# A DeltaNet-and-MLP kernel: x·w_in by eleven products of tiles instead of twelve, with shared sums on GpSimd

## The chip, the core and the metric

The kernel runs on one core of a Trainium2 chip. The core has engines that work side by side and wait for each other by semaphores: TensorE (PE in the profile; PEld is its weight load), VectorE (DVE), ScalarE (ACT), GpSimd (POOL) and the queue that issues most transfers (SP). Each engine takes its own instructions in the order in which the program wrote them. TensorE writes into PSUM; here DVE and ACT take results out of PSUM, and GpSimd works on SBUF alone.

The metric is the device time of one execution, in microseconds (us). Before the change three runs gave 692.02, 690.9 and 692.4, median 692.02.

## What is computed

```python
# attention: B, H, S, D = 4, 8, 768, 48, a state matrix per (batch, head)
for t in range(S):
    y[:, :, t] = q_t @ state
    state += beta_t * outer(k_t, v_t - state^T k_t)       # k normalised
# MLP on the 3072 tokens x 384 features of y
h = x @ w_in                                               # 384 -> 2048
g = h * clip(h + 3, 0, 6) / 6                              # hardswish
out = g @ w_out                                            # 2048 -> 384
```

## The kernel before, in words

**Attention.** The 768 steps are cut into 24 chunks of 32 tokens; one chunk of all four batches fills 128 partitions. For a chunk `t`, `prep` (L474) scales the keys on GpSimd (`kb`, L479), makes the mask times beta there (`mb`, L457), transposes k and q on TensorE (L495), multiplies them (`sc`, L516), lets DVE cut out the triangles `L` and `LB` (L527), and lets GpSimd make `bkb` (L467). Chunks are inverted in groups of four: `inverse` (L715) is a long chain of DVE instructions on two SBUF tiles (`pr` L728 and `A` L733, 60 of them, with a transpose of about 2 us at either end, L447 and L451). `chain` (L756) is the recurrence: `ks` (L775), `R` on DVE (L788), `pz` (L877), `Z` on ACT (L882), `su` and `py` on TensorE, the state on DVE (L908), and the output rows `y` (DVE L788 and L831), turned by TensorE (`yt`, L841) into `xT`, the input of the MLP.

**MLP.** Two chunks make a block of 256 tokens; there are 12 blocks, counted from 0 in the code. `up(blk)` (L935) makes h^T: for each of 16 slices of 128 features, three fp32 products of a 128x128 weight tile with 256 columns of `xT`. The profile counts two matmul instructions for each fp32 product. ACT makes relu(h/6 + 1/2) (L955) and DVE min(·,1)·h (L958), into `g`. `down_by_seven(blk)` (L1032, from block 2) makes g·w_out by seven products of half matrices instead of eight, each of 8 products of 192 columns (L1052). It needs 16 sums of halves of g (L1038, 128x256, two SBUF inputs), made on DVE between the products, and combines the results in `o` (L1059, L1062). Products are made in the order 4, 2, 1, 5, 7, 6, 3. PSUM for all this is a ring of four banks (`pm`); `ks`, `su` and `sc` have two others (`pc`).

**Order.** Everything is recorded in program order by hand. Up to chunk 4 the string `ORDER` (L22) names the pieces one by one. Then the loop at L1262 runs a step for each chunk from 5 on: 15 units, each of which takes pieces of the chain and of `prep` by the table `plan`, one unit of `mlp_units` (L1117: `down` of a block and `up` of the next, 30 units together), and two or three pieces of the running inverse or norms. `prep` runs six chunks ahead, so after chunk 17 it has nothing more to do; the last block's `up` and `down` stand alone at the end. The inverse of the next group starts in the second step of a group of four, fills the third and ends in the fourth.

```python
            for u in range(NU):
                if u in plan:
                    plan[u]()
...
                take(units)
                settle(1)
...
                take(fill, 2 + (u % 3 == 0))
```

Of the kernel before, what the change touches and what calls it, by code (L numbers as in the profile page):

```python
# [35 lines left out]
x4 a*2 u b6 x4 q a u c*2 u ru c w ru a gu u p8 a u gu a q*2 n9 k q c a u a w c p6 ru q s c p7 p6  # L36
m7 a p7 u m8 k c h3 u ru gu b7 p8 h3 p8 c k h4 p8 gu c*2 p8 a u h4 ru gu u k ru gu u y4 p8 x4*2 u
y4 p8 i2*2 u i2 v i2*3 ru i2 u a i2*2 gu a ru u i2*3 h4 i2 gu b8 i2 k n9 q i2*2 k u q k*2 v k*2 ub
k*2 v h4 i2*2 u rb i2 gb n9 i2 u i2 v i2 ru i2 gu i2 u ru i2*3 v q gu i2 c n9 u k i2 u i2 u ru gu
q ru i2 gu i2 k n9 v i2 u h4 y4 i2 v*2 i2 n9 u y4 i2 q u*2 i2 u n9 ru i2*3 q k gu q*2 i2 n9 q i2*3  # L40
n9 u k n9 q e i2*4 ru u gu y4 h4 e n9 u y4 k n9 k*2 i2 k*5 i2*2 k*3 ru k ru gu i2 u gu p9 u e i2 u
i2*5 e u i2*4
"""


# [1 line left out]
def kernel(  # L47
# [62 lines left out]
        return 0 if g == 0 else G0 + (g - 1) * GS  # L110


    NKB, NQB, NBKB, NLB, NKQ = 2, 4, 8, 8, 7
    kbufs = [persist.tile([P, H, DP], FP32, name=f"kb{i}") for i in range(NKB)]
    qbufs = [persist.tile([P, H, DP], FP32, name=f"qb{i}") for i in range(NQB)]
    bkbufs = [persist.tile([P, H, DP], FP32, name=f"bkb{i}") for i in range(NBKB)]
    kfs, vfs = {}, {}

    def tokens(ap, b, t):
# [5 lines left out]
    def needs(*what):  # L125
        assert past.issuperset(what), (what, set(what) - past)
# [33 lines left out]
                    past.add(("q", t))  # L160
                yield

    NVF = 3

    def load_v(t):
        if t < N:
# [284 lines left out]
        nc.vector.transpose(out=turn(inverted(g)), in_=problems(A))  # L451

    def mask(t):
        mb = mbs[t] = work.tile([P, 2, NP, 2, C], FP32, name="mb")
        needs("beta")
        for e in range(2):
            nc.gpsimd.tensor_tensor(  # L457
                out=mb[:, e],
                in0=beta_tok[:, t, e:H:2].unsqueeze(2).unsqueeze(3).to_broadcast([P, NP, 2, C]),
                in1=mask2[:].unsqueeze(1).to_broadcast([P, NP, 2, C]),  # L460
                op=ALU.mult,
            )
        yield

    def scaled(t):
        needs(("kb", t), *pad(t), *([("bkb", t - NKB)] if t >= NKB else []))
        nc.gpsimd.tensor_tensor(  # L467
            out=bkbufs[t % NBKB][:, :, 0:D], in0=kbufs[t % NKB][:, :, 0:D],
            in1=beta_tok[:, t, 0:H].unsqueeze(2).to_broadcast([P, H, D]), op=ALU.mult,
        )  # L470
        past.add(("bkb", t))
        yield
# [65 lines left out]
    def product(t):  # L538

        assert G == 8 and C == 4 * G and 4 * H * C == NP * B * 2 * C
        needs("blocks")
        LT = X(t)
        by = "p (h w) -> p h w"

        ring("KQ", NKQ, ("x", t))
        VYTF = work.tile([P, 4, H * C], FP32, name="VY", tag="KQ", bufs=NKQ)  # L550
        VY, V, Y, T, F = VYTF[:, 0:2], VYTF[:, 0, :], VYTF[:, 1, :], VYTF[:, 2, :], VYTF[:, 3, :]

        keys = []

        def times(rhs):

            n = rhs.shape[1]
            key = ("pi", t, len(keys))
            ring("pm", NPM, key)
            keys.append(key)  # L560
            ps = psM.tile([P, 2, H * C], FP32, name="pi", tag="pm")
            for h in range(H):
                w = slice(C * h, C * h + C)
                for b in range(B):
                    nc.tensor.matmul(
                        ps[rows(b), 0:n, w], lhsT=T[rows(b), w], rhs=rhs[rows(b), :, w],
                        start=True, stop=True, skip_group_check=True,
                        tile_position=(C * b, C * b),
                    )
            return ps  # L570

        def plus(ps):
            nc.vector.tensor_tensor(out=Y, in0=Y, in1=ps, op=ALU.add)

        nc.vector.tensor_tensor(
            out=V.rearrange("p (h n w) -> p h n w", h=H, w=G),
            in0=LT.rearrange("p h (n w) -> p h n w", w=G),
            in1=blocks[:].unsqueeze(1).unsqueeze(3).to_broadcast([P, H, C // G, G]),
            op=ALU.mult,
        )  # L580
        nc.vector.transpose(out=T, in_=V)
        yield
        ps = times(VY[:, 0:1, :])
        yield
        nc.vector.tensor_tensor(
            out=Y.rearrange(by, w=C), in0=eye[:].unsqueeze(1).to_broadcast([P, H, C]),
            in1=V.rearrange(by, w=C), op=ALU.subtract,
        )
        nc.vector.tensor_tensor(
            out=F.rearrange(by, w=C), in0=LT, in1=V.rearrange(by, w=C), op=ALU.subtract  # L590
        )
        yield
        nc.scalar.activation(out=V, in_=ps[:, 0, :], func=ACTF.Copy)
        yield
        nc.vector.transpose(out=T, in_=ps[:, 0, :])
        read(*keys)
        yield
        ps = times(VY)
        yield
        nc.vector.transpose(out=T, in_=ps[:, 0, :])  # L600
        plus(ps[:, 1, :])
        read(*keys)
        yield
        ps = times(VY[:, 1:2, :])
        yield
        plus(ps[:, 0, :])
        nc.vector.transpose(out=T, in_=Y)
        read(*keys)
        yield
        ps = times(F.unsqueeze(1))  # L610
        yield
        nc.scalar.activation(out=V, in_=ps[:, 0, :], func=ACTF.Copy)
        yield
        nc.vector.transpose(out=T, in_=ps[:, 0, :])
        read(*keys)
        yield
        ps = times(VY)
        yield
        nc.vector.transpose(out=T, in_=ps[:, 0, :])
        nc.vector.tensor_tensor(out=Y, in0=Y, in1=ps[:, 1, :], op=ALU.subtract)  # L620
        read(*keys)
        yield
        ps = times(VY[:, 1:2, :])
        yield
        nc.vector.scalar_tensor_tensor(
            out=LT, in0=Y.rearrange(by, w=C), scalar=-1.0,
            in1=ps[:, 0, :].rearrange(by, w=C), op0=ALU.mult, op1=ALU.subtract,
        )
        read(*keys, ("x", t))
        past.add(("X", t))  # L630
        yield
# [3 lines left out]
    def join(t):  # L635
# [4 lines left out]

        needs("corner")
        LT = X(t)
        ring("KQ", NKQ, ("x", t))
        tiles = work.tile([P, 4, H, C], FP32, name="VY", tag="KQ", bufs=NKQ)
        T, S, T2 = (tiles[:, i] for i in range(3))

        def times(name, m, k):
# [108 lines left out]
    def chain(t, whole=True):  # L756
# [5 lines left out]
        KQ, LB = KQs.pop(t), LBs[t]  # L762
        if t > 0:
            needs(("state", t - 1))
        bkb = bkbufs[t % NBKB]

        def of_state():
            ph = [banks("ks", t, i) for i in range(2)]
# [91 lines left out]
        if t == 0:  # L860
            R = vfl
        else:
            needs("parity")
            Rt = work.tile([P, DM], FP32, name="R", bufs=1)
            for x, ph, into in ((0, even, vfl), (1, odd, Rt[:])):
                plus(Rt[:], ph, parity[:, x, 0:1], into)
            R = Rt[:]
            yield
# [9 lines left out]
        past.add(("pz", t))  # L878
        yield 1
        read(("pz", t))  # L880
        Zt = work.tile([P, DM], FP32, name="Z", bufs=1)
        nc.scalar.activation(out=Zt[:], in_=pz[:, 0:DM], func=ACTF.Copy)  # L882
        Z = zs[t] = Zt[:]
        past.add(("Z", t))
# [15 lines left out]

        needs(("bkb", t))
        su = update() if t < N - 1 else []
        if whole:
            take(outs[t])
        yield
# [29 lines left out]
    def up(blk, half_of=None):  # L935
# [5 lines left out]
        for f in range(NFC):  # L941
# [27 lines left out]
                past.add(("up", blk))  # L969
            yield  # L970

    def to_dram(t, o):
        for b in range(B):
            r0 = b * S + t * C
            eng = nc.scalar if t >= N - CB and b % 2 else nc.sync
            eng.dma_start(out=out[r0 : r0 + C, :], in_=o[rows(b ^ 1)])
# [55 lines left out]
    def down_by_seven(blk):  # L1032
# [2 lines left out]

        def sums(op, out, a, b, fs):
            for f in fs:
                nc.vector.tensor_tensor(out=A(f, *out), in0=A(f, *a), in1=A(f, *b), op=op)  # L1038

        lo, hi, A11, A12, A21, A22 = (0, 2), (4, 6), (0, 0), (0, 1), (1, 0), (1, 1)  # L1040
        o = mlp.tile([128, CB, DM], FP32, name="o", bufs=1)
# [20 lines left out]
            nc.vector.tensor_tensor(out=out, in0=a, in1=b, op=ALU.add)  # L1062

        settle()
        product(4, A22, T4, 0)
        yield
        product(4, A22, T4, 1)
        copy(C21, 4, -1.0)
        yield
        product(2, A12, B21, 0)  # L1070
        yield
        product(2, A12, B21, 1)
        copy(C11, 2)
        sums(ALU.add, A22, A21, A22, lo)
        yield
        product(1, A11, B11, 0)
        sums(ALU.add, A22, A21, A22, hi)
        yield
        product(1, A11, B11, 1)
        copy(u, 1)  # L1080
        sums(ALU.subtract, A21, A11, A21, lo)
        yield
        product(5, A22, T1, 0)
# [33 lines left out]
    def mlp_units():  # L1117
# [3 lines left out]
        for f in range(0, NFC, WF):  # L1121
# [3 lines left out]
            for _ in range(WF):  # L1125
                next(u1)
                yield
        for blk in range(1, N // CB):
            if blk < FIRST:
                for c in range(CB):  # L1130
                    for f in range(0, NFC, WF):
                        if c == 0:
                            needs(*(("read", ("ph", blk, f + i, None)) for i in range(2)))
                        down(blk, c, f)
                        yield
            else:
                yield from down_by_seven(blk)
            if blk + 1 < N // CB:
                for n, _ in enumerate(up(blk + 1)):
                    if blk + 1 == FIRST and n >= HF:  # L1140
                        drain(rest)
                        if n % 2:
# [15 lines left out]
            pass  # L1158

    NU = 15  # L1160
    LA = 6
    LE = 4
    LS = G0 + GS
    gens = {}

    def made(name, make, ok=True):
# [177 lines left out]
```

## Time and profile before

The profiled execution took 688.24 us; its span, from the first to the last instruction, is 686.5 us, so 1.7 us lie around it.

| engine | busy us | share of the span | instructions |
|---|---|---|---|
| TensorE (PE) | 647.2 | 94% | 11208 |
| weight load (PEld) | 567.8 | 83% | 11208 |
| VectorE (DVE) | 467.8 | 68% | 1210 |
| ScalarE (ACT) | 238.9 | 35% | 476 |
| GpSimd (POOL) | 95.2 | 14% | 147 |

In the views below a row of the timeline reads: start in us, duration in us, engine, line, operation, output<-input, shape, how many were merged into the row, and in brackets how long the engine sat idle before it and what released it. Rows of one engine can overlap by a few hundredths, and matmuls by more, because they are pipelined: the pace of a run of matmuls is taken from start to start, not from one duration.

### The profile page before, as it was taken

Reading aid. Unit: us, or ns where it says so; the run is one execution under the profiler, and the core shown is the slowest. Engines: PE = TensorE matmul, PEld = TensorE weight load, DVE = VectorE, ACT = ScalarE, POOL = GpSimd, SP = SyncE. Lnnn points to the kernel's source line nnn. Section 1 sums busy time; section 2 is a strip of 40 time slices with the busy share of each in tenths; the row PEclk is TensorE's granted clock in tenths of the full one; section 3 lists DMA queues with packets and bytes.
Section 4 is the critical chain, followed back from the end, with each engine's and each line's share of the span. In section 5 each row is a group of like instructions: output and inputs, shape, how many; then the busy total and the mean of one; then the engine's idle time right before and its main releaser. Section 6 shows DMA issues by size and latency. Waiting matters only on the chain.

```text
span 686.5 us, 25308 instructions
## 1 busy us (share of the span) xinstructions
PE 647.2 (94%) x11208; PEld 567.8 (83%) x11208; DVE 467.8 (68%) x1210; ACT 238.9 (35%) x476; POOL 95.2 (14%) x147
## 2 busy tenths in 40 slices
PE   2668989999999999999999999999999999999997
PEld 2458877776688988988988988988988989989997
DVE  5898776888746997846985745985546985445242
ACT  5995677421233232232232232232232132132220
POOL 6241022203521100400101302100000000000000
PEclk9977899999999999999999999999999999999999
DMA  7987125412041030031030030020020020000000
GB/s 197 246 199 189 37 66 139 82 24 47 15 79 30 2 68 6 2 78 29 3 64 9 3 71 2 2 61 1 3 48 2 2 48 2 25 3 1 25 0 24
DMA packets 88494, 33.20 MB, mean 48 GB/s; under 512 B 80160, under 2 KB 83232, under 8 KB 88384
## 3 DMA queue, kind: packets, MB, share of 16 engines
q1 hardware_dynamic: 88128, 31.29, 20.5%
q8 instruction: 88, 1.44, 0.9%
q10 hardware_dynamic: 256, 0.30, 0.2%
q14 instruction: 22, 0.18, 0.1%
HBM read 26.84 MB, written 4.72 MB: 46 GB/s over the span
## 4 chain that ended last, share of the span: by engine, by line
PE 73%; DVE 12%; DMA 7%; issue 3%; ACT 2%; SPq 1%; POOL 0%; DVEq 0%; ACTq 0%; POOLq 0%
PE ph L947 33%; PE po L1052 21%; PE po L987 4%; PE ks L775 3%; PE py L796 2%; PE su L893 2%; PE pz L796 2%; DVE g L1038 2%; DMA w_out<-in_moe_w_in_dram 2%; DVE pr L728 2%; DVE A L733 2%; PE sc L516 2%; PE pt L495 2%; DMA spare<-in_moe_w_in_dram 2%; DMA qb<-in_q_dram 1%
## 5 line engine op out<-in xcount | busy, mean ns | idle before, releaser
L947 PE MATMUL ph<-xT,w_in 128*128 128x256 f32 (+1 forms) x1248 | 271.3, 371 | 3.8 <-DVE g L958 2.3
L947 PEld LDWEIGHTS ph<-xT,w_in 128*128 128x128 f32 x1248 | 222.3, 194 | 33.1 <-DVE g L958 3.5
L955 ACT ACTIVATE g<-ph,halves 128x256 f32<-128x256 f32 (+1 forms) x208 | 94.4, 456 | 198.1 <-PE ph L947 196.5
L958 DVE SCALAR_TENSOR_TENSOR g<-g,ph 128x256 f32<-128x256 f32 (+1 forms) x208 | 81.7, 396 | 100.1 <-ACT g L955 99.9
L1052 PE MATMUL po<-w_out,g 128*128 128x192 f32 x640 | 113.3, 328 | 0.0
L1052 PEld LDWEIGHTS po<-w_out,g 128*128 128x128 f32 x640 | 103.9, 190 | 0.5
L1052 PE MATMUL po<-spare,g 128*128 128x192 f32 x480 | 84.8, 330 | 0.0
L1052 PEld LDWEIGHTS po<-spare,g 128*128 128x128 f32 x480 | 78.1, 190 | 1.8
L1038 DVE TENSOR_TENSOR g<-g 128x256 f32<-128x256 f32 x160 | 65.5, 463 | 0.5 <-PE po L1052 0.4
L733 DVE TENSOR_TENSOR A<-A,pr 128x30 f32<-128x30 f32 (+9 forms) x150 | 52.2, 348 | 3.4
L728 DVE TENSOR_TENSOR pr<-A 128x30 f32<-128x30 f32 (+9 forms) x150 | 51.1, 341 | 3.1
L334 ACT ACTIVATE spare<-spare,places 128x768 uint16<-128x768 uint16 (+1 forms) x56 | 52.4, 940 | 1.9 <-DMA spare<-in_moe_w_in_dram 1.0
L987 PE MATMUL po<-w_out,g 128*128 128x384 f32 x128 | 45.6, 493 | 0.0
L479 POOL TENSOR_TENSOR kb<-kf,inv 128x384 f32<-128x384 f32 x24 | 23.0, 958 | 155.2 <-PE pt L495 69.9
L457 POOL TENSOR_TENSOR mb<-beta_tok,mask 128x256 f32<-128x256 f32 x48 | 34.9, 748 | 66.6 <-DVE LB L527 66.5
L1059 ACT ACTIVATE o<-po 128x192 f32<-128x192 f32 x40 | 13.2, 330 | 88.1 <-PE po L1052 88.1
L503 ACT ACTIVATE KQ<-pt 128x512 f32<-128x512 f32 x48 | 28.1, 594 | 42.5 <-PE pt L495 42.0
L987 PEld LDWEIGHTS po<-w_out,g 128*128 128x128 f32 x128 | 23.2, 190 | 12.3
L775 PEld LDWEIGHTS ks<-state,KQ 64*64 64x64 f32 x1472 | 24.3, 136 | 10.2 <-issue 9.0
L845 ACT ACTIVATE xT<-yt 128x384 f32<-128x384 f32 x24 | 11.7, 486 | 57.3 <-PE yt L841 57.3
L775 PE MATMUL ks<-state,KQ 64*64 64x48 f32 x1472 | 27.7, 222 | 3.7 <-issue 2.9
L788 DVE SCALAR_TENSOR_TENSOR y<-ks,parity,y 128x192 f32<-128x192 f32 x46 | 17.0, 412 | 19.3 <-ACT y L812 19.3
(109 smaller groups left out, 594.8 us busy)
## 6 DMA issues: line engine op xcount, KB each, us to landing
kf<-in_k_dram SPq DMA_DIRECT2D x96, 48.0 KB, 2.7
qb<-in_q_dram SPq DMA_DIRECT2D x96, 48.0 KB, 3.0
vf<-in_v_dram SPq DMA_DIRECT2D x96, 48.0 KB, 2.2
out_dram<-o SPq DMA_DIRECT2D x92, 48.0 KB, 1.6
spare<-in_moe_w_in_dram SPq DMA_DIRECT2D x4, 768.0 KB, 6.5
w_out<-in_moe_w_in_dram SPq DMA_DIRECT2D x4, 768.0 KB, 5.9
w_out<-in_moe_w_out_dram SPq DMA_DIRECT2D x4, 768.0 KB, 6.5
spare<-in_moe_w_out_dram SPq DMA_DIRECT2D x4, 768.0 KB, 5.8
```

The lines of the kernel that those rows point to most:

```text
L334: nc.scalar.activation(out=z, in_=z if n else d.bitcast(I16)[:, :, :, 3], func=func, bias=places[:, n : n + 1], scale=scale,)
L457: nc.gpsimd.tensor_tensor(out=mb[:, e], in0=beta_tok[:, t, e:H:2].unsqueeze(2).unsqueeze(3).to_broadcast([P, NP, 2, C]), in1=mask2[:].unsq ...
L503: nc.scalar.activation(out=KQ[:, :, 0:4:3, :] if j == 0 else KQ[:, :, 1:3, :], in_=pt[:].rearrange("q p (x y c) -> q (p x) y c", y=2, c=C) ...
L728: nc.vector.tensor_tensor(out=pv, in0=A[:, j + 1 :, j].unsqueeze(2).to_broadcast([n, w, j]), in1=A[:, j, 0:j].unsqueeze(1).to_broadcast([n ...
L733: nc.vector.tensor_tensor(out=A[:, j + 1 :, 0:j], in0=A[:, j + 1 :, 0:j], in1=pv, op=ALU.subtract)
L775: nc.tensor.matmul(ph[y][c, e, D * p : D * p + D], lhsT=KQ[r, p * B // 2 + b // 2, 2 * y : 2 * y + 2, :].rearrange("k y c -> k (y c)"), rh ...
L947: nc.tensor.matmul(ph[:, cols], lhsT=w_in[:, s, f * 128 : (f + 1) * 128], rhs=xT[:, s, cols], start=(s == 0), stop=(s == NKT - 1),)
L955: nc.scalar.activation(out=g, in_=ph, func=ACTF.Relu, bias=half, scale=1.0 / 6.0)
L958: nc.vector.scalar_tensor_tensor(out=g, in0=g, scalar=1.0, in1=ph, op0=ALU.min, op1=ALU.mult)
L987: nc.tensor.matmul(pos[c][:], lhsT=gs[blk, f // 2][:, f % 2, c * P : (c + 1) * P], rhs=w_out[:, f, :], start=(f == 0), stop=(f == NFC - 1),)
L1038: nc.vector.tensor_tensor(out=A(f, *out), in0=A(f, *a), in1=A(f, *b), op=op)
L1052: nc.tensor.matmul(ps[n][:], lhsT=A(f - f % 2, *a)[:, f % 2], rhs=b[:, f], start=(f == 0), stop=(f == HF - 1),)
```

## The change

It has four parts.

1. **Eleven products.** From block 2 (`UF = 2`) `up_by_eleven` takes the place of `up`. Two slices of features and two halves of the tokens make a 2x2 problem; in the first two of the three slices of the inner dimension seven tile products do for eight, and the third has its four: eleven of 128x128 by 128 columns, where before there were six of 256 columns. Four results of a pair `j` lie in one PSUM bank. `begin(j)` makes four products; ACT copies the whole bank into `g` (128x512), GpSimd makes three sums there (128x128). `end(j)` adds seven products into the same bank; DVE adds the shared parts (128x128 and 128x256); ACT copies the first quarter, then makes the relu of all four quarters from `g` into a tile `ro` (of the tag `o`, one buffer); DVE makes min·h (128x512, both inputs in SBUF now). `begin` runs two pairs ahead of `end`. The units of a block are 16 as before.
2. **Sums of the inputs.** GpSimd makes sums of w_in once (`weight_sums`, 16 instructions of 128x256, one for each unit of block 1's `down`) and sums of x for each block (`token_sums`, 4 of 128x128, ahead of the last two units of the `down` before).
3. **g's sums on GpSimd.** The 16 sums of `down_by_seven` go from DVE to GpSimd, and product 1 is made first: 1, 4, 2, 5, 7, 6, 3.
4. **Room and order.** The sums of w_in need 12 KB a partition. `VY`, one `bkb` and every second early mask live in that tile until then; masks have one buffer later, `vf` two for three, `KQ` six for seven, `LB` seven for eight, and `Z` takes over R's buffer. `ORDER` loses four units of `mlp_units` and four loads of v.

```diff
-    NKB, NQB, NBKB, NLB, NKQ = 2, 4, 8, 8, 7
+    NKB, NQB, NBKB, NLB, NKQ, NVY = 2, 4, 8, 7, 6, 2
+    sums_in = persist.tile([P, 3, NPR, P], FP32, name="sums_in")
...
-    NVF = 3
+    NVF = 2
...
-        Zt = work.tile([P, DM], FP32, name="Z", bufs=1)
+        Zt = Rt if t > 0 else work.tile([P, DM], FP32, name="R", bufs=1)
...
+    def weight_sums():
+        for j in range(0, NPR, 2):
+            r = slice(j, j + 2)
+            plus_minus(S1[:, r], W21[:, r], W22[:, r], ALU.add)
+            yield
...
+    def token_sums(blk):
+        plus_minus(T1x, B12, B11, ALU.subtract)
+        plus_minus(T2x, B22, T1x, ALU.subtract)
+        plus_minus(B12, B22, B12, ALU.subtract)
+        plus_minus(T4x, B21, T2x, ALU.subtract)
...
+        def begin(j):
+            mm(ph, 0, W11[:, j], B11, start=True)
+            mm(ph, 1, S1[:, j], T1x)
+            mm(ph, 2, W21[:, j], T3x)
+            mm(ph, 3, S2[:, j], T2x)
+            nc.scalar.activation(out=gt, in_=ph[:], func=ACTF.Copy)
+            plus_minus(gt[:, 1], gt[:, 1], gt[:, 2], ALU.add)
+            plus_minus(gt[:, 2], gt[:, 0], gt[:, 1], ALU.add)
+            plus_minus(gt[:, 0], gt[:, 0], gt[:, 3], ALU.add)
...
+        def end(j):
+            mm(ph, 0, W12[:, j], B21)
+            mm(ph, 1, S4[:, j], B22)
+            mm(ph, 2, W22[:, j], T4x)
+            mm(ph, 0, W13[:, j], B31)
+            mm(ph, 1, W13[:, j], B32)
+            mm(ph, 2, W23[:, j], B31)
+            mm(ph, 3, W23[:, j], B32, stop=True)
+            nc.vector.tensor_tensor(out=gt[:, 3], in0=ph[:, 3], in1=gt[:, 2], op=ALU.add)
+            nc.vector.tensor_tensor(
+                out=gt[:, 1:3], in0=ph[:, 1:3],
+                in1=gt[:, 0].unsqueeze(1).to_broadcast([128, 2, P]), op=ALU.add,
+            )
+            def first():
+                nc.scalar.activation(out=gt[:, 0], in_=ph[:, 0], func=ACTF.Copy)
+                nc.scalar.activation(out=r, in_=g, func=ACTF.Relu, bias=half, scale=1.0 / 6.0)
+                def rest():
+                    nc.vector.scalar_tensor_tensor(
+                        out=g, in0=r, scalar=1.0, in1=g, op0=ALU.min, op1=ALU.mult
+                    )
...
         def sums(op, out, a, b, fs):
             for f in fs:
-                nc.vector.tensor_tensor(out=A(f, *out), in0=A(f, *a), in1=A(f, *b), op=op)
+                nc.gpsimd.tensor_tensor(out=A(f, *out), in0=A(f, *a), in1=A(f, *b), op=op)
...
+            sums = weight_sums() if blk == UF - 1 else iter(())
+            for n, _ in enumerate(downs(blk)):
+                next(sums, None)
+                if n == last and UF <= blk + 1 < N // CB:
+                    drain(sums)
+                    token_sums(blk + 1)
+                yield
```

## The prediction

> **What bounds the kernel now.** I read the page first (busy shares, slices), then the span cut into stretches, then the timeline of the last block, where nothing but the MLP runs, and last the stretches where DVE inverts a group. Page, second part:
>
> ```profile
> PE   2668989999999999999999999999999999999997
> POOL 6241022203521100400101302100000000000000
> PEclk9977899999999999999999999999999999999999
> ```
>
> From the tenth slice on PE is full at full clock and POOL nearly empty. The stretch from 250 to 643 us gives PE 391.3 busy of 393.0, and the waits of PE in it sum to 1.7 us, all for the DVE instruction at L958. So the end is set by the sum of PE's work; a product saved is time saved unless a new wait takes it. DVE is the next engine. Over three steps of the chain (chunks 14, 15 and 16):
>
> ```profile
> 400.30:426.90 26.60, 26.60 (x431) 23.01 (x429) 14.02 (x36) 9.52 (x20) 3.82 (x6) 1.00 0.20 35
> 426.90:452.50 25.60, 25.60 (x446) 24.01 (x445) 23.25 (x63) 5.25 (x12) 3.34 (x4) 1.00 0.03 7
> 452.50:476.70 24.20, 23.33 (x411) 19.97 (x411) 18.04 (x52) 8.62 (x18) 0.00 (x0) 1.00 0.19 38
> ```
>
> The columns are stretch, length, then busy PE, PEld, DVE, ACT, POOL. Where the inverse runs with `down` (second row) DVE is busy 23.25 of 25.6 us; in the step behind it PE waits 0.87 us (458.27, for DVE).
>
> **The change, part by part.**
>
> *Products.* The pace of a run is the distance of its first and last start, divided:
>
> ```profile
> 643.48 20.88 PE L947 MATMUL ph<-xT,w_in 128*128 128x256 f32 x96
> 664.20 2.76 PE L1052 MATMUL po<-spare,g 128*128 128x192 f32 x16
> ```
>
> ```profile
> 559.93 5.45 PE L947 MATMUL ph<-xT,w_in 128*128 128x256 f32 x24
> ```
>
> ```profile
> 60.88 4.29 PE L947 MATMUL ph<-xT,w_in 128*128 128x128 f32 x36 [0.30 <-DVE g L958]
> ```
>
> 96 instructions of 256 columns from 643.48 to 664.20: 20.72 us, 0.2158 each. The same run behind the small products of the chain (x24: (5.45-0.38)/23 = 0.220) pays 0.105 once at its start. With 128 columns (block 0, full clock): (4.29-0.275-0.105)/35 = 0.1117, with 0.275 the median duration of one. I take 0.1115. `up` then costs 2x88x0.1115 = 19.62 for 20.72, **-1.10 a block, -11.0 for ten**. Ends: the line through 192 columns (0.162) and 256 gives 0.1083 at 128, 19.06, -16.6 in all; the run of 36 without the deduction, 0.1147, gives 20.19, -5.3. T1x, T2x and T4x are read as pieces of 16 columns with gaps, which no row here shows as a moving operand; the second end holds that.
>
> *ACT and DVE in `up`.* A pair takes PE 22x0.1115 = 2.45 us. ACT: 0.59 (128x512, L503), 0.28 (128x128, L679) and a relu of 128x512, by the line through 0.364 (128) and 0.473 (256) 0.69: 1.56, under PE. DVE, start to start: about 0.20 and 0.33 for the adds (L667, L527), 0.61 for min·h of 512 (estimate, from 0.346 for 256 at L1038 and about 0.47 for 384 at L1022), 1.14 for 0.66 before: +3.9 us a block, against -16x0.346 = -5.5 in `down`. PSUM: a bank waits for ACT's first quarter, which stands behind DVE's adds; begin runs two pairs ahead, so about one pair (2.4 us) of lateness costs nothing; what is lost behind that is the group term below.
>
> *GpSimd.* Medians: 128x384 0.83 (L479), 128x256 mostly 0.61 to 0.66 (L457), so 1.7 ns a column and 0.18 fixed; 128x128 about 0.40. A block takes 16x0.61 + 24x0.40 + 4x0.40 = 21.0 us of some 47. In `down` four sums (2.45) must go with each product (16x0.162 = 2.60): with the work of the chain on PE (about 5.7 us a step) hidden; alone, in the last block, hidden by 0.15 a product and by the half product's head start. At over 0.65 a sum that cover goes, and each 0.1 more would cost the last block up to 1.6 us. kb, the masks and bkb stand in the same queue: they wait for chunks done 8 units earlier, so nothing queues behind an open wait. token_sums (1.6) run under product 3 (2.6). In the step with norms, sq and DVE's ss take turns; R may come 0.8 us late there, twice, which I put into the start term.
>
> *Contention.* This is what speaks against the change:
>
> ```profile
> 383.74 0.83 POOL L479 TENSOR_TENSOR kb<-kf,inv 128x384 f32<-128x384 f32 x1 [2.72 <-DVE inv L409]
> 383.79 1.06 DVE L1038 TENSOR_TENSOR g<-g 128x256 f32<-128x256 f32 x1
> ...
> 385.75 1.41 POOL L457 TENSOR_TENSOR mb<-beta_tok,mask 128x256 f32<-128x256 f32 x2 [1.18 <-DVE LB L527]
> 385.85 3.60 DVE L1038 TENSOR_TENSOR g<-g 128x256 f32<-128x256 f32 x8
> ```
>
> One DVE sum beside kb takes 1.06 (0.42 alone); eight beside two masks take 3.60 for 2.85. So a GpSimd instruction takes from DVE's two-input SBUF work 0.64 of its 0.83, or about 0.38 of its 0.61 to 0.70. Instructions with one input in PSUM show nothing of it: at 160.80 L958 keeps 0.41 beside a mask. [...]
>
> *One group* (chunks 15 and 16 as the measure, ks 426.99 to yt 473.65). From DVE's queue up to y (ends 471.59) go 16 sums, 5.5, and 11 of L958, 3.6. To it come five pairs of adds, 2.7, and five of min·h, 3.1: net -3.3. GpSimd adds 16 sums x 0.39 and 19 small ones x 0.20 = 10.0, if each met a two-input instruction; the inverse and min·h are about 0.65 of DVE's time there: +6.5. Net DVE +3.2. PE's work in the stretch falls by about 1.9 (1.6 of it, as the units stand three later in the step). Slack before: y came 2.1 early at yt, DVE idled about 2.3 us in chunk 16 (1.08 at 460.85), and 0.87 was already lost. Lateness 3.2+1.9-2.1 = 3.0, of which the idle time takes some; I take **+1.5 a group, +6.0** for four groups (chunks 6 to 21). Ends: 0 if the idle time takes all, +5 if none and the adds are hit too: 0 to +20.
>
> *Start.* Four units (16 matmuls, 159.97 to 165.23) move from under the second inverse into chunk 5's step. DVE ends that inverse at 166.8 and needs 1.4 for R, and PE now has some 7 us of other work until then: about 0.6 of wait. 16 weight sums (9.8 us), four sq and L1022's two-input sums share one step, and block 2 waits for the last of them: 0 to 3. VY with two buffers holds a memset and so the masks behind it: 0 to 1. I take **+1.5**, ends 0 and +5.
>
> *At nothing:* Z in R's buffer (R waits for ks, which already waits for su); vf, KQ, LB (their readers are a step back; vf lands 2.2 us after issue, a step ahead); relu in `o` (the output's issue ends 2.6 us after the last sum at 397.67, the first relu comes some 4 us after; without that cover about 1 us a block).
>
> **Sum.** -11.0 + 6.0 + 1.5 = -3.5 on 688.24, so 684.7 for the profiled execution. The runs' median is 3.8 above it: **688.5**.
>
> **Rivals.** (a) *Ports decide, slower.* In the third step of each group GpSimd's 16 sums and DVE's inverse take turns, R, y and the adds come late, and PE waits at pz, yt and begin. At the upper end, 5 a group: -11.0 + 20 + 1.5 = +10.5, 702.5. It decides from (11.0-1.5)/4 = 2.4 a group on. For: 23.25 of 25.6 busy already, 1.06 for 0.42. Against: the sums leave DVE, and DVE has idle time in the fourth step. (b) *Clean.* No waits: -11.0, 681.0; with the better pace 675.4. For: 1.7 us of PE waits in 393. Against: no slack in the third step. (c) *The products don't save it.* At 0.1147 or with slow strided reads: -5.3 + 7.5 = +2.2, 694.2.
>
> **How the numbers follow.** This kernel can't be told from no change within 0.2% (1.4 us). Forecast (small gain, 682 to 690.6) 0.43; clean, below 682, 0.10; between 690.6 and 693.4 0.10; rival (a) 0.29; rival (c) 0.08. Faster 0.53, same 0.10, slower 0.37. Range 679 to 702: it leaves out the better half of the clean case and the worst of (a).
>
> **What would show it.** In the last block's `up` 176 instructions from first to last start in 19.6; above 20.2 the product term is wrong. GpSimd's sums at 0.6 to 0.65 in the last block, 0.7 to 0.9 beside the inverse. PE idle in the third and fourth step of each group, released by DVE or POOL, 2 to 3 us together; over 3.3 makes (a) true. Idle before `pz` of chunk 5 and `up` of block 2 under 3. No idle in the steps without inverse; if PE waits there too, for POOL or ACT, a wait that I cost at nothing is wrong.

## The result and the profile after

The changed kernel takes **738.54 us** (median of 4 runs, 734.9 to 740.2) against 691.53 (4 runs): ratio 1.067, 95% interval 1.063 to 1.071. The prediction was a small gain, 688.5, with 702.0 as its upper end; the change is slower by 47 us. The profiled execution has a span of 738.5 us and a mean granted TensorE clock of 0.954 (before: 686.5 and 0.985). Ahead of the ks of chunk 5 both show 0.94; from there to the end the clock is 0.96, before 1.00.

The rows of the page's second part that answer to those shown of before, busy tenths and granted clock in 40 slices:

```profile
PE   2569989996998988999798799988999798999997
POOL 6220232027555845644844456653654734634645
PEclk9977999997999999899999999999999989999999
```

PE was full from the tenth slice to the end; now it has holes of 1 to 3 tenths that come back every few slices, and the clock dips in some of them. POOL, nearly empty before, is half busy throughout.

Steps of the chain, chunks 9, 10, 11 and 19 (stretch, length, then busy PE, PEld, DVE, ACT, POOL, clock):

```profile
282.80:317.16 34.36, 28.93 (x465) 27.63 (x464) 13.72 (x33) 7.67 (x18) 22.49 (x34) 0.90 0.04 8
317.16:341.26 24.10, 24.10 (x489) 23.29 (x488) 14.83 (x36) 11.06 (x22) 10.80 (x23) 1.00 0.35 67
341.26:373.84 32.58, 28.07 (x465) 26.73 (x464) 30.60 (x59) 7.35 (x17) 21.71 (x30) 0.95 0.05 9
567.72:600.02 32.30, 26.56 (x393) 25.38 (x392) 28.97 (x60) 6.37 (x15) 16.86 (x23) 0.89 0.04 8
```

Chunk 10 is as hoped: PE has no idle time and the step is shorter than before (25.5). In chunk 9 (the norms) and in 11 and 19 (third steps of a group) PE is idle for 4.5 to 5.7 us, and its own work takes longer at a lower clock. From chunk 5 on the idle times of PE over 0.5 us sum to 43.4 us; before they summed to 2.7.

The step with norms. DVE's timeline, start, duration and, in brackets, the idle time ahead of it with its releaser:

```profile
287.76 0.54 DVE L404 TENSOR_REDUCE ss<-sq 128x8 f32<-128x384 f32 x1
289.24 0.55 DVE L404 TENSOR_REDUCE ss<-sq 128x8 f32<-128x384 f32 x1 [0.94 <-POOL sq L400]
290.73 0.55 DVE L404 TENSOR_REDUCE ss<-sq 128x8 f32<-128x384 f32 x1 [0.94 <-POOL sq L400]
291.20 0.73 DVE L810 SCALAR_TENSOR_TENSOR R<-ks,parity,vf 128x192 f32<-128x192 f32 x2
291.85 0.73 DVE L810 SCALAR_TENSOR_TENSOR R<-ks,parity,R 128x192 f32<-128x192 f32 x2
292.50 0.28 DVE L1073 TENSOR_TENSOR g<-ph,g 128x128 f32<-128x128 f32 x1
```

ACT behind it:

```profile
293.36 0.28 ACT L1080 ACTIVATE g<-ph 128x128 f32<-128x128 f32 x1 [4.22 <-DVE g L1074]
293.94 0.72 ACT L1084 ACTIVATE o<-g,halves 128x512 f32<-128x512 f32 x1 [0.30 <-DVE g L1087]
295.88 0.32 ACT L408 ACTIVATE root<-ss,places 128x32 f32<-128x32 f32 x1 [1.22 <-DVE ss L404]
296.11 0.58 ACT L525 ACTIVATE KQ<-pt 128x512 f32<-128x512 f32 x1
296.58 0.57 ACT L834 ACTIVATE y<-ks,parity 128x384 f32<-128x384 f32 x1
```

And PE:

```profile
292.41 1.03 PE L818 MATMUL pz<-R,X 32*32 32x48 f32 x64 [1.66 <-DVE R L810]
297.21 1.18 PE L538 MATMUL sc<-KQ 64*32 64x64 f32 x64 [3.77 <-ACT y L834]
298.32 5.05 PE L1199 MATMUL po<-spare,g 128*128 128x192 f32 x16
```

One late engine hands its lateness round. Three `ss`, each waiting for its `sq`, stand in front of R; R is late for pz. The adds of the last pair of `up` stand behind R; ACT's first quarter waits 4.22 us for them. The relu, the norms' `root` (which waits 1.22 us for the fourth `ss`), the copy of q's transposes and y queue up behind that. `sc` needs the PSUM that y frees: 3.77 us. Then sixteen instructions that take 2.76 at full clock take 5.05.

The third step of a group, on POOL, DVE and PE:

```profile
353.37 12.87 POOL L1185 TENSOR_TENSOR g<-g 128x256 f32<-128x256 f32 x16 [7.56 <-PE po L1199]
```

```profile
363.32 0.81 DVE L750 TENSOR_TENSOR pr<-A 128x238 f32<-128x238 f32 x1
364.16 0.81 DVE L755 TENSOR_TENSOR A<-A,pr 128x238 f32<-128x238 f32 x1
364.89 1.01 DVE L932 TENSOR_TENSOR state<-state,su 128x384 f32<-128x384 f32 x2
365.82 0.54 DVE L853 TENSOR_TENSOR y<-y,py 128x384 f32<-128x384 f32 x1
...
371.94 0.40 DVE L750 TENSOR_TENSOR pr<-A 128x228 f32<-128x228 f32 x1
```

```profile
366.51 0.52 PE L863 MATMUL yt<-ident,y 128*128 128x128 f32 x3 [2.94 <-DVE y L853]
366.86 1.99 PE L1199 MATMUL po<-w_out,g 128*128 128x192 f32 x8
368.65 3.96 PE L1199 MATMUL po<-spare,g 128*128 128x192 f32 x16
372.44 1.46 PE L1199 MATMUL po<-w_out,g 128*128 128x192 f32 x8
```

While the sums run (0.80 each) thirteen steps of the inverse take 0.76 to 0.92, those shown 0.81; once GpSimd is done such a step takes 0.40. y stands behind them in DVE's queue, and yt waits 2.94 us (2.95 and 5.74 in chunks 15 and 19). The eight instructions behind it take 1.99 and the sixteen 3.96, where 1.46 and 2.76 are usual.

### The profile page after: what moved, and what is told of

It reads as the page before. It is cut to its first block, busy times and chain, and to the rows that moved or that the text cites. A ratio compares the mean times of both kernels' runs of the same rounds, so it can differ in the third digit from the quotient of the medians.

```text
span 738.5 us, 27699 instructions
## 1 busy us (share of the span) xinstructions
PE 657.8 (89%) x12008; PEld 605.5 (82%) x12008; DVE 494.5 (67%) x1130; ACT 281.8 (38%) x556; POOL 359.8 (49%) x603
## 4 chain that ended last, share of the span: by engine, by line
PE 49%; DVE 19%; POOL 3%; issue 2%; ACT 1%; DVEq 0%; POOLq 0%; ACTq 0%
PE ph L1043 20%; PE po L1199 18%; DVE pr L750 5%; DVE A L755 5%; DVE g L1087 3%; PE po L1134 2%; PE ks L797 2%; PE sc L538 1%; DVE g L1074 1%; DVE R L810 1%; POOL g L1008 1%; DVE state L932 1%; PE py L818 1%; PE pz L818 1%; PE yt L863 1%
## 5 line engine op out<-in xcount | busy, mean ns | idle before, releaser
L1008 POOL TENSOR_TENSOR g<-g 128x128 f32<-128x128 f32 x240 | 113.5, 474 | 163.7 <-ACT g L1057 150.7
L1043 PE MATMUL ph<-xT,w_in 128*128 128x128 f32 x1120 | 177.5, 282 | 10.2 <-DVE y L853 9.2
L1043 PEld LDWEIGHTS ph<-xT,w_in 128*128 128x128 f32 x1120 | 150.4, 195 | 13.7 <-DVE y L853 10.2
L1185 POOL TENSOR_TENSOR g<-g 128x256 f32<-128x256 f32 x160 | 118.6, 776 | 69.2 <-PE po L1199 61.8
L1057 ACT ACTIVATE g<-ph 128x512 f32<-128x512 f32 x80 | 47.8, 597 | 114.9 <-PE ph L1043 114.9
L1087 DVE SCALAR_TENSOR_TENSOR g<-o,g 128x512 f32<-128x512 f32 x80 | 63.5, 794 | 9.1 <-ACT o L1084 9.1
L1084 ACT ACTIVATE o<-g,halves 128x512 f32<-128x512 f32 x80 | 57.8, 722 | 17.5 <-DVE g L1087 14.2
L1043 PE MATMUL ph<-beta_tok,sums_in 128*128 128x128 f32 x320 | 62.4, 277 | 0.0
L501 POOL TENSOR_TENSOR kb<-kf,inv 128x384 f32<-128x384 f32 x24 | 22.3, 931 | 68.0 <-PE ph L971 35.6
L971 PE MATMUL ph<-xT,w_in 128*128 128x128 f32 (+1 forms) x288 | 50.5, 331 | 0.7 <-ACT spare L347 0.7
L1043 PEld LDWEIGHTS ph<-beta_tok,sums_in 128*128 128x128 f32 x320 | 49.1, 194 | 0.0
L971 PEld LDWEIGHTS ph<-xT,w_in 128*128 128x128 f32 x288 | 43.7, 206 | 5.1 <-ACT spare L347 0.8
```

The source lines that it names most:

```text
L971: nc.tensor.matmul(ph[:, cols], lhsT=w_in[:, s, f * 128 : (f + 1) * 128], rhs=xT[:, s, cols], start=(s == 0), stop=(s == NKT - 1),)
L1008: nc.gpsimd.tensor_tensor(out=out, in0=a, in1=b, op=op)
L1043: nc.tensor.matmul(ph[:, n], lhsT=w, rhs=x, start=start, stop=stop, skip_group_check=True)
L1057: nc.scalar.activation(out=gt, in_=ph[:], func=ACTF.Copy)
L1084: nc.scalar.activation(out=r, in_=g, func=ACTF.Relu, bias=half, scale=1.0 / 6.0)
L1087: nc.vector.scalar_tensor_tensor(out=g, in0=r, scalar=1.0, in1=g, op0=ALU.min, op1=ALU.mult)
```

## The experiments

Two theories stood at the start. **A:** GpSimd's work lengthens DVE's instructions with both inputs in SBUF (a step of the inverse takes 0.81 beside the sums, 0.40 without them), so R, the adds and y come late and PE waits. **C:** the eleven products' own work on DVE and ACT is too long for where it stands, and GpSimd is innocent. B was A at a dearer price, an assumption: DVE shut out for the whole of a sum. Theories Q, D and K came from the first four runs. Times are medians; each run was taken beside the kernel before on the same chip, whose medians were 690.4 to 690.7. Differences between runs are taken from the medians; by their ratios to the kernel before they come out about the same or up to 2.3 us smaller.

**Where the sums are made** (e1: `nc.gpsimd` to `nc.vector` in `sums`; e2: the kernel before with the opposite edit and product 1 first).

```diff
-                nc.gpsimd.tensor_tensor(out=A(f, *out), in0=A(f, *a), in1=A(f, *b), op=op)
+                nc.vector.tensor_tensor(out=A(f, *out), in0=A(f, *a), in1=A(f, *b), op=op)
```

> The changed kernel with g's sixteen sums of a block back on DVE; everything else as changed. Theory A (shared access): beside the inverse one sum on GpSimd lengthens one two-input DVE instruction by about 0.42 us, and on DVE it costs 0.35 itself, so moving it back gains DVE at most 0.07 x 16 = 1.1 us a group, four groups, with the granted clock behind it: 730 to 738 us, and pr and A of the inverse at 0.34 to 0.41 again in the third steps. Rival B (a GpSimd instruction shuts DVE out for its whole 0.75 us): 16 x 0.4 = 6.4 us a group come back, the waits at yt go, 705 to 715. Rival C (GpSimd's sums are innocent; the waits come from the eleven products' own work on DVE and ACT): DVE has 5.5 us a group more to do, 745 to 760.

> The kernel before with one part of the change alone: g's sums on GpSimd, product 1 first; the up product keeps its twelve products. Theory A: DVE loses 5.5 us of sums a group and pays 16 x 0.42 = 6.7 for GpSimd's, net +1.2 a group in the third step, where PE has some slack: 691 to 697, with pr and A at about 0.8 beside the sums. Rival B: 16 x 0.75 - 5.5 = +6.5 a group, so waits of some 4 us in each third step and a lower granted clock behind them: 708 to 720. Rival C: the inverse keeps its pace and DVE is freer, 689 to 691.5.

Measured: e1 730.67 (ratio 1.056, 1.051 to 1.062), e2 697.53 (1.008, 1.005 to 1.011). Both are A's: a sum costs DVE nearly the same wherever it is made, 0.39 on DVE itself (160 in 62.8 us, e1) and about 0.42 beside the inverse on GpSimd; B, and C's 745 to 760, fall. e2 is 0.5 over A's range. Its third step, in POOL's, DVE's and PE's timelines:

```profile
331.36 6.48 POOL L1038 TENSOR_TENSOR g<-g 128x256 f32<-128x256 f32 x8
```

```profile
336.45 0.80 DVE L728 TENSOR_TENSOR pr<-A 128x228 f32<-128x228 f32 x1
...
349.18 0.40 DVE L728 TENSOR_TENSOR pr<-A 128x228 f32<-128x228 f32 x1
```

```profile
343.00 0.52 PE L841 MATMUL yt<-ident,y 128*128 128x128 f32 x3 [0.80 <-DVE y L831]
355.16 2.86 PE L947 MATMUL ph<-xT,w_in 128*128 128x256 f32 x12 [1.72 <-DVE g L958]
```

The same doubling of the same step of the inverse, in a kernel with no eleven products at all: so it is the sums on GpSimd that do it. They alone cost 7 us, not 47.

**The squares on ScalarE, and no sums at all.**

```diff
-            if g < 4:
+            if True:
                 nc.scalar.activation(out=sq[:], in_=kf[:, i0 + i], func=ACTF.Square)
```

> The changed kernel with the squares of the keys (sq, read by the norms) on ScalarE in every group, so that GpSimd makes none. Theory A: in the steps with norms (chunks 5, 9, 13) ss no longer waits 0.94 a time for sq on GpSimd, R is in time, the wait at pz (4.6, 1.7, 1.7 us) goes and the one at sc behind it (1.1 to 3.8) shrinks, with it one drop of the granted clock each: 722 to 732. Rival C (ACT's queue is what is late): four squares more on ACT make the wait at sc longer, 737 to 744.

> The changed kernel without g's sums: neither GpSimd nor DVE makes them, so what the down product computes is not the reference's from block two on; all else runs. Theories A and B: DVE gets the 16 x 0.42 or more of a group back, the waits at yt in the third steps (2.9 to 5.7 us) and at ph in the fourth (2.0 to 2.9) go, and the drop of the clock behind them: 4 x 6 to 8 us less, 707 to 716. If it falls to about the time of the sums on DVE, the sums never decided. Rival C: 732 to 739, the waits stay, since GpSimd's small adds and the DVE and ACT work of the eleven products are still there.

Measured: e3 739.66 (1.070), e4 720.07 (1.042). e3 is A's miss: `ss` now waits 0.59 instead of 0.94, but the squares stand in ACT's queue behind the relu that is late itself, and PE waits as before (1.64 at pz and 3.77 at sc in chunk 9). So it isn't who makes the squares. e4, 4 us over the range of A, takes away the waits at yt, and leaves those at sc (3.69, 2.42) and ph. Without any sum 30 us of the loss remain: most of it had another cause than the sums. What A and C both lacked was **order**.

**Order: the norms later (Q), the inverse spread (D), both, and both with the sums on DVE.** In the loop over units:

```diff
# e5, e7, e8
+                if i == 0 and u < 5:
+                    continue
# e6, e7, e8
-                if i == 1 == ready[0] and 5 < u < 12:
-                    continue
-                take(fill, 2 + (u % 3 == 0))
+                slow = ready[0] == 1 and (i, u) >= (1, 6)
+                take(fill, 1 + (u % 3 != 0) if slow else 2 + (u % 3 == 0))
```

> The changed kernel with the norms of a later group (sq and ss) begun five units later in their step, behind R and the last adds of the up product in DVE's queue; their work is the same. Theory Q (order on DVE: three ss, each waiting 0.6 to 0.9 us for its sq, whoever makes it, stand in front of R and of the last adds; ScalarE's first quarter, relu, the copy of q's transposes and y stand behind the adds, and TensorE's sc behind those): in chunks 9 and 13 the waits at pz (1.66) and sc (3.8 and 2.4) go with the drop of the clock behind them, 2 x 5 to 8 us, and some of the 5.8 in chunk 5: 718 to 728. Rival C (the eleven products' own adds, relu and min times h are too long for the units in front of sc, norms or not): sc waits stay above 1.5, 732 to 738.

> The changed kernel with the inverse of groups 4 to 6 spread evenly: it begins in unit 6 of the second step without the pause of six units, and takes 1.67 instead of 2.33 of its steps a unit. Theory D (density: in the third step GpSimd's sums lengthen each step of the inverse by 0.42, and y stands behind seven or eight of them; what counts is how many steps of the inverse are ahead of y): the waits at yt in chunks 11, 15 and 19 (2.9, 2.9, 5.7) fall by half or go, and those at ph in the fourth step (2.0 to 2.9) shrink: 10 to 20 us with the clock, 718 to 728. Rival: work is only moved, the second step of the group, which has no wait now, gets one of 1 to 3 us at its adds, and the last steps of the inverse come late for the next group's pz: 733 to 742.

> The changed kernel with both: norms five units later and the inverse spread evenly. The sums of g stay on GpSimd. If the two causes are separate, their gains add: 698 to 718. If each only uncovers the other's wait, it stands within 3 us of the better of the two.

> Norms later, inverse spread, and g's sums on DVE as in the kernel before, so that GpSimd keeps only the shared parts of the eleven products. Theory A (a sum costs DVE 0.42 from GpSimd and 0.35 on itself, so that its place hardly matters) says within 6 us of the same kernel with the sums on GpSimd; with all waits gone it would be about 681 to 690. If the sums on GpSimd cost much more than that (they also run beside work other than the inverse), 10 us or more below it.

Measured: e5 724.35 (1.048), e6 717.16 (1.038), e7 705.05 (1.020), e8 700.51 (1.013; 1.010 to 1.016). Against 738.54 that is 14.2, 21.4 and 33.5 us: Q and D hold, and their gains add up (35.6); e6 is 0.8 better than its range. e8 is 4.5 below e7, so A's small difference for the sums holds too. DVE's timeline in e5, chunk 9:

```profile
282.59 1.36 DVE L1087 SCALAR_TENSOR_TENSOR g<-o,g 128x512 f32<-128x512 f32 x1
283.88 0.73 DVE L810 SCALAR_TENSOR_TENSOR R<-ks,parity,vf 128x192 f32<-128x192 f32 x2
```

No `ss` stands between them, R starts at once, pz no longer waits and `sc` waits 0.66 instead of 3.77 (yt, 1.79, is new). In e6 the third step of chunk 11 is

```profile
340.22:367.69 27.47, 26.39 (x464) 25.05 (x464) 25.87 (x47) 7.33 (x17) 20.34 (x27) 1.00 0.05 10
```

27.47 for 32.58 at full clock, with steps of the inverse at 0.80 all the same: GpSimd takes as much from each, there are fewer of them ahead of y. A little of the rival shows too: waits of 1.21 at ph in chunks 10 and 14 are new.

**The granted clock (K).** Dummy products in front of the waits; e12 has about half as many as e9.

```diff
+    def warm(x, n):
+        for _ in range(n):
+            nc.tensor.matmul(x, lhsT=ident[:], rhs=ident[:], start=True, stop=True, skip_group_check=True)
...
+            warm(pt[:, 0, :], WARM_YT.get(t, 0))
             for s in range(NKT):
```

> The changed kernel with dummy products (identity by identity, 128 columns, into columns of PSUM that nobody reads, or that the transposes overwrite) on TensorE in front of its eleven longest waits: 30 ahead of pz in chunk 5, 8 to 25 ahead of sc in chunks 7, 9 and 13, 20 to 44 ahead of yt in 11, 15 and 19, 10 to 18 behind py in 8, 12, 16 and 20; each fills the wait but for 0.6 to 1 us. Nothing else is late or early by it. Theory K (a gap of some 2 us lowers the granted clock, and the slower matmuls behind it cost 1.7 to 2.7 us each, some 20 us in all): the mean clock rises from 0.954 to 0.98 or more and the time falls to 718 to 728, although no wait is taken away. Rival (the clock falls for another reason, or the dummies only push real work back): the clock stays under 0.965 and the time at 735 to 745.

> The changed kernel with half as many dummy products in front of the same waits (a product of four-byte numbers goes out as two instructions of 0.11 us, so 20 of them took 4.5 us where the wait was 2.9, and what was won in the clock was lost in dummies). Theory K (a gap of about 2 us lowers the granted clock, and that costs some 15 to 20 us of the 48): no wait is longer than before, the clock in the middle of the run stays at full, 718 to 728. Rival (the slower products behind a wait are themselves hidden, since the next wait is for DVE and only begins later): the clock rises all the same, and the time stays within 4 us of 738.5.

Measured: e9 738.93 (1.069) at a clock of 0.977, e12 726.75 (1.053; 1.049 to 1.058) at 0.981. e9's time was the rival's and its clock nearly K's, since the dummies were twice too long: 40 instructions, 4.6 us, for a wait of 2.9. From chunk 5 on the clock is 0.99 in both, where the changed kernel has 0.96. e12 decides it: K's range. PE at chunk 11's yt:

```profile
366.36 0.55 PE L874 MATMUL yt<-ident,y 128*128 128x128 f32 x3 [0.85 <-DVE y L863]
366.75 1.47 PE L1212 MATMUL po<-w_out,g 128*128 128x192 f32 x8
368.05 2.76 PE L1212 MATMUL po<-spare,g 128*128 128x192 f32 x16
```

The same y is late by as much, but PE has worked until 0.85 us before it, and the 8 and 16 instructions behind it take 1.47 and 2.76 instead of 1.99 and 3.96. Useless work gains 11.8 us (9.5 by the ratios), so some 10 to 12 us of the loss were the clock's. The gain is net, since not every wait stayed as it was: pz in chunk 9 waits 2.21 for 1.66, and yt in chunk 7 waits 2.46 where it didn't wait.

**Taking the waits away one by one, and a control.** e10: e8, with `sc` a unit later, the inverse from unit 10 of the second step and a pause at the head of the third. e11: the kernel before with the edits of e7.

```diff
# e10
+                plan[4] = lambda: take(ch)
+                if i == 0 and u < 5 or i == 2 and u < 4 and ready[0] == 1:
+                    continue
```

> The eleven products with the waits taken away one by one: g's sums on DVE, norms five units later, the inverse begun at unit 10 of the second step at about 2.2 of its steps a unit with a pause in the first four units of the third step, and sc a unit later, behind other work of TensorE. If order on DVE and ACT is all that stood between the eleven products and their gain, 684 to 692 (681 with no wait at all in the prediction's sum, and 5 to 8 us for chunks 5 to 8, which keep theirs). If waits come back in other steps, 695 to 702, as the version before it.

> The kernel before with the same two changes of order as the version with sums on DVE (norms five units later, inverse spread evenly): a control that says what the eleven products, their shared parts on GpSimd and the moved start cost by themselves. Theory: the kernel before had no waits for these to remove (1.7 us of PE waits in 393), so 688 to 692; the eleven products then cost 9 to 12 us in that order, at chunks 5 to 8 and in the third steps. Rival (the new order costs by itself): 695 or more.

Measured: e10 703.50 (1.019; 1.015 to 1.023), e11 687.30 (0.996; 0.994 to 0.999). e10 misses, and is slower than e8: the waits moved. PE's timeline of e10:

```profile
332.25 2.87 PE L1199 MATMUL po<-w_out,g 128*128 128x192 f32 x16 [1.56 <-ACT g L1080]
369.83 0.84 PE L916 MATMUL su<-R,bkb 32*64 32x48 f32 x60 [1.71 <-DVE LB L549]
```

With `sc` later, LB is late for su, and the first down product waits for the PSUM that ACT's first quarter frees. e11 says that the new order costs the kernel before nothing and gains it 0.1 to 0.6%, a little more than expected. In that order the eleven products, with their shared parts, buffers and moved start, cost 13 us (12 by the ratios).

**What the 13 us are, and where the products pay.** e13: e8 without the three `plus_minus` in `begin`. e14: e8 with eleven products in the last two blocks alone, and three of the four units back at the start.

```diff
# e14
-    UF = 2
+    UF = 10
-            last = (NFC if blk < FIRST else NFC - 2) - 3
+            last = (NFC if blk < FIRST else NFC - 2) - 2
```

> The version with g's sums on DVE, norms later and the inverse spread, without the three additions of each pair by which GpSimd forms the shared parts (so the up product from block two on is not the reference's). It asks what still costs the eleven products 13 us against the kernel before in the same order of work, and 24 against their own sum. Theory A (GpSimd's small additions, 24 a block of 0.5 us, lengthen min times h from 0.68 to 1.2 and the steps of the inverse by 0.2 to 0.4 each): 687 to 692. Rival (the rest is the start, chunks 5 to 8, and the order of adds, first quarter and relu on DVE and ACT): 697 to 701.

> Eleven products for the last two blocks alone, where no inverse and no norms run; twelve for the others, g's sums on DVE, the norms later and the inverse spread, and three of the four units of the first down product back beside the second inverse. Theory: the saving of 1.1 us a block stands wherever DVE has time, so 2 us under the kernel before in the same order (687.3): 683 to 687. If the eleven products' setting (their buffers, the shared parts of the weights) costs by itself, 690 or more.

Measured: e13 695.22 (1.006; 1.003 to 1.009), e14 **684.48** (0.992; 0.989 to 0.995). e13 lies between the two theories: the shared additions cost 5.3 us. Without them min·h takes 0.70 us on average for 0.79 (chunks 5 to 19) and a step of the inverse 0.38 for 0.40, and DVE's adds no longer wait for GpSimd (6.3 us in e8); the run doesn't part the two ways. The other 8 against e11 are elsewhere, and 3.95 of them are the one wait at pz of chunk 5. There the sums of w_in run beside the end of the second inverse: its last six steps take 0.62 to 0.75 us, in e14, which makes no such sums there, 0.19 to 0.25. e14 is 0.8% below the kernel before. PE's timeline of its last `up`, first row and the row behind it:

```profile
640.45 0.39 PE L1043 MATMUL ph<-xT,w_in 128*128 128x128 f32 x2
...
660.16 2.77 PE L1199 MATMUL po<-w_out,g 128*128 128x192 f32 x16
```

19.71 us from the one to the other, where the kernel before takes 20.72. From the ks of chunk 21 to the end e14 is 0.2 us shorter than before (109.8 for 110.0) with one unit, some 1.35 us, more left to do: about 1.5 of the 2.2 us that two blocks should save. That is the smaller part of its gain of 0.8%, 5.6 us. e11 puts the order at 2.7; what is left lies within the interval, and e14's and e11's intervals just overlap.

## Why the prediction was wrong, point by point

- *Products, -1.10 a block*: nearly right. In the last block `up` takes 19.77 us for 20.72, -0.95; reading T1x, T2x and T4x in pieces costs nothing that shows. Rival (c) falls.
- *GpSimd hidden in the last block*: right. Sixteen sums in 11.1 us, 0.69 each, more than the 0.65 at which the cover was said to go, and PE doesn't stall.
- *Contention, 0.38 a sum*: right in size. It is 0.42 for a step of the inverse, and thirteen steps met the sixteen sums. Had a step waited out a whole sum, as B has it, it would have taken about 1.1 (an estimate: the 0.69 of a sum in the last block and the step's own 0.40). The rows give 0.81, and moving the sums back gains 8 us (e1), not the 23 to 33 of B.
- ***One group, +1.5* is the step that failed.** It added up DVE's work over two steps (net +3.2), took off slack and idle time from anywhere in them, and called the rest the wait. But a wait is set by what stands in front of one instruction. The slack of 2.1 was that of the fourth step's y (chunk 16). The y of the third step, behind which the sums land, had 0.5 before (DVE's row and PE's):

```profile
445.95 0.55 DVE L831 TENSOR_TENSOR y<-y,py 128x384 f32<-128x384 f32 x1
...
446.98 0.49 PE L841 MATMUL yt<-ident,y 128*128 128x128 f32 x3
```

From the ks of chunk 15 to the end of this y DVE was busy 18.0 of 19.5 us; now it is busy 23.6 of 25.2. That is 5.6 more against 0.5 of slack, and PE waits 1.66 at sc and 2.95 at yt. The size was wrong too: up to the y of chunk 16 DVE's work grew by 9.2, not 3.2 (57 steps of the inverse now fall into the stretch, 51 before). Chunks 15 and 16 together take 60.6 us for 52.3. e6 leaves the work as it is, changes the order alone, and gains 21 us.

- *Rival (a)* came out by its own sign (over 3.3 us in the third and fourth step): 2.94 at yt and 2.04 at ph in one group, besides 1.57 at sc. But the sums on GpSimd, which it names as the cause, are worth 8 us moved back (e1) and 18 left out (e4). At 702.5 it is 36 short. The runs show that the two engines lengthen each other's instructions; that "ports" are the reason, as its name has it, no run shows.
- *Start and norms, +1.5*: failed in the same way. "R may come 0.8 us late" was counted as 0.8; it was 1.66 at pz, and 3.77 at `sc` three engines on. e5 puts the norms' order at 14 us. In chunk 5 the wait was 4.64, not 0.6. R was said to need 1.4 us from the end of the inverse at 166.8; the rows of before show three `ss` ahead of it, and R begins at 170.56:

```profile
170.09 0.55 DVE L391 TENSOR_REDUCE ss<-sq 128x8 f32<-128x384 f32 x1 [0.94 <-POOL sq L387]
170.56 0.73 DVE L788 SCALAR_TENSOR_TENSOR R<-ks,parity,vf 128x192 f32<-128x192 f32 x2
...
172.54 0.88 PE L796 MATMUL pz<-R,X 32*32 32x48 f32 x64
```

Now R begins at 171.18, hardly later, but PE, without the four units (5.3 us), is at pz about that much earlier and waits. The four units also put every later piece of the MLP four places back against the chain: two pairs of `up` now stand behind the ks of chunk 9. No run parts this shift from the eleven products' own adds.

- *At nothing, ACT in `up` (1.56 of 2.45)*: wrong. The sum fits, the order doesn't: before, the relu waited for PE alone; now the first quarter and the relu wait for DVE, and the copy for `sc` waits behind them. It shows in chunks 7, 11 and 15 too, 1.57 to 1.85 us.
- *No idle in the steps without inverse*: this sign turned out against the prediction. Chunk 22 has no idle time, nor have chunks 10, 14 and 18, into which three steps of the inverse fall. But chunks 9 and 13 have no inverse, only norms, and PE waits 5.4 and 4.1 us there; chunk 17 has neither and waits 0.67 at `sc`. The waits at `sc` end with ACT: the cost put at nothing.
- *The granted clock*: in no step. e12 shows 12 us of it, and the table below puts slower matmuls at some 21.

Why 738.5 and not 691, in the order in which it was taken away: order 33.5, the sums' place 4.5, the shared additions 5.3. These include the clock's share, and 8 us against e11 are left. Where they lie shows in the stretch from the ks of chunk 5 to the end. It leaves out the start, whose length changes from execution to execution: three profiles with the same start (e2, before, e11) reach that ks at 161.3, 165.2 and 170.8.

| | us | PE busy | PE not busy | granted clock |
|---|---|---|---|---|
| before | 521.3 | 514.5 | 6.8 | 1.00 |
| changed | 578.2 | 531.0 | 47.3 | 0.96 |
| e13 | 532.5 | 513.8 | 18.8 | 1.00 |
| e11 | 519.2 | 514.1 | 5.1 | 1.00 |

In the changed kernel PE is idle 40.5 us more. It is busy 16.5 more: the four units add 5.3, and ten blocks at -0.95 take off 9.5, so some 20.7 (an estimate from these rows) are matmuls that ran slower. The saving is there, then: chunks 21 and 22, without waits, take 46.85 us for 47.81. In e13 against e11 it is eaten up: 13.7 us more of idle time, the 3.95 at pz and others of 0.6 to 1.5, and by the same sum 3.8 of slower matmuls.

## What to carry to other kernels

A DVE nearly full in one step isn't priced by a sum over a group: list, for each instruction that TensorE waits for, what stands in front of it in its queue, and give each of those its stretched duration. Moving work to GpSimd freed next to no time on DVE while DVE ran two-input work in SBUF (a sum took 0.39 on DVE, and 0.42 from the inverse beside it); where DVE has nothing of the kind to do it might pay, which no run here tested. An exchange that saves matmuls and adds steps on two other engines belongs first in the stretches where those are idle, as the last two blocks here (e14).

## What the runs showed of the hardware

- A wait of TensorE can cost more than its length. After 2.94 us without a matmul eight instructions took 1.99 for 1.46 and the next sixteen 3.96 for 2.76; after 5.74 us eight took 2.77. Waits of 1.56 to 1.66 us at chunks 11 and 15 and in e10 were followed by the usual 2.87 for sixteen. Length alone doesn't settle it: in the four us behind a wait the granted clock was 0.60 after 1.85 us (chunk 7) and 0.65 after 2.04 (chunk 12), but 1.00 after 2.21 (chunk 20). With dummy products in the wait, and 0.85 us of it left, the eight took 1.47 and the sixteen 2.76 (e12, chunk 11).
- GpSimd and DVE lengthened each other's instructions: sixteen sums of 0.80 (0.69 in the last block, where no inverse runs) beside thirteen steps of 0.76 to 0.92 (0.34 to 0.41 alone).
- A dummy product of four-byte numbers, 128 by 128 by 128, goes out as two instructions and takes 0.23 us (40 in 4.63).
